# Cached-attention decode block: maxima per key group, shared normalisation, and work moved from TensorE to VectorE in ten queries

## The chip, the cores and the metric

The kernel runs on one core of a Trainium2 chip. The metric is the device time of one execution in microseconds (us), lower is better. Before the change the median of three runs is 1307.19 us (1306.52 to 1307.53).

## What is computed

A decoding step for two sequences (batch 2), model width 448: layer normalisation, attention of one new token per sequence over a cache of 8192 keys in 16 heads of 256, a residual sum, a second layer normalisation, a bilinear feed-forward layer of width 1792 and a second residual sum. All in 32-bit floats. Cut to what matters:

```python
q = (layernorm(x) @ wq).reshape(B, 1, 16, 256).transpose(0, 2, 1, 3)   # B = 2
scores = einsum("bhqd,bhkd->bhqk", q, k_cache) * 256 ** -0.5             # 8192 keys
o = einsum("bhqk,bhkd->bhqd", softmax(scores), v_cache)
h = x + o.transpose(0, 2, 1, 3).reshape(B, 1, 4096) @ wo
n = layernorm(h)
out = h + ((n @ w_gate) * (n @ w_up)) @ w_down
```

There are 32 pairs of a head and a sequence, called queries here and numbered i = 2 * head + sequence. Each has its own 8 MB of keys and 8 MB of values, which are read once: 537 MB in all, out of 561 MB that the kernel reads.

## The kernel before, in words

**Layout.** The 8192 keys of a query are cut into four groups of 2048. The key tile has the 128 partitions as one half of the head dimension (index `c` in 0, 1 for the two halves), then the four groups, then the 2048 keys of a group. The score tile `s` lies in PSUM as 128 x 2048: partitions 32g to 32g+31 hold group g, all 32 the same numbers, since the query is copied into 32 columns (`queries`, L193). The value tile `v` is 128 x 8 x 2048: partition 32g + r, slot o holds value dimension 32o + r of the keys of group g. So VectorE forms the output as a product of each slot with the 128 x 2048 tile of weights `p`, summed along the keys.

**Loop over the queries** (from L228). For each query i:

- SyncE (SP) issues the load of the keys (L84) into a buffer that exists once (`kbuf`, 64 KB a partition), then the load of the values (L91) into one of two buffers (`vbuf`). Each is one DMA of 8 MB. The issue of the next query's keys waits in SP's program until the last reader of the present keys is done, and what stands behind it on SP waits too.
- TensorE makes the scores (L206): four column tiles of 512 keys, two halves `c` and four groups, 32 matmuls of 128 x 32 weights; the four groups lie in four strips of the array's columns and run side by side. In the trace each 32-bit matmul is two records.
- VectorE takes the maximum along the 2048 keys (L242). TensorE turns the 128 numbers into a row (L244), VectorE takes their maximum (L246), TensorE spreads it to all partitions (L248), ScalarE copies it (L250). Only then ScalarE makes `p` = exp(s - max) and its sum (L252).
- VectorE forms the eight products with `v`, one instruction a slot (L259, SCALAR_TENSOR_TENSOR with an accumulator that is read out by a second, short instruction).
- After every second query `head_out` adds up the groups and divides by the sum of the weights for this head (L211 to L223); it stands behind the scores of the next query.

The tile framework turns every dependence between engines into a semaphore; each engine runs its own list in program order.

**Ends.** Before the loop come the first normalisation and the query projection out of `wq_t`, during which the first keys are under way. Behind the loop SP issues the loads of the output projection (`wo_t`, into the key buffer), gate and up weights (`gu_t`, into the value buffer of query 30) and down weights (`wd_t`, into that of query 31). The output projection, the second normalisation (L303 to L335) and the feed-forward layer follow. Gate and up products lie in banks 0 and 1 of one PSUM tile `ff`; the transposed products `hm_ps` in banks 2 and 0.

Of the kernel before, what the change touches and what calls it, by code (L numbers as in the profile page):

```python
# [20 lines left out]
GK = SK // G  # L21
# [15 lines left out]

WO_CUTS = (6, 11, 14, 15)


LAYOUT = (
    (slice(0, P), slice(0, DC - 1), slice(0, DC - 1)),
# [6 lines left out]
def tile_decode_block(  # L49
# [9 lines left out]
    wd: bass.AP,  # L59
    out: bass.AP,  # L60
):

# [46 lines left out]
    xr = const.tile([P, DC + 1, B, 16], F32, name="xr")  # L109
    nc.gpsimd.memset(xr[:, DC - 1 :], 0.0)  # L110
    oT = const.tile([P, H, 2, B], F32, name="oT")
    acc_ps = ps_1.tile([P, D], F32, name="acc_ps")
    nc.vector.memset(acc_ps, 0.0)

# [57 lines left out]

    qT = const.tile([P, 2, G, 2, 2, B], F32, name="qT")
    q_ps = ps_s.tile([P, 4, MM], F32, tag="s", name="q_ps")
    q_sb = one.tile([P, 2, MM], F32, tag="p", name="q_sb")
    for k in range(2):
        project(
            q_ps[:, k], wq_t, HD, (MM,) * 4, [k * BATCH + g * MM for g in range(4)],
# [9 lines left out]
            q_ps[:, 2 + k].rearrange("p (n g b r) -> p n g b r", n=4, g=G, b=B)[..., 0],  # L188
        )

    def queries(h):
# [9 lines left out]
    def scores(s, q, b, kt):  # L201
        for j in range(GK // MM):
            at = slice(j * MM, (j + 1) * MM)
            for c in range(2):
                for g in range(G):
                    nc.tensor.matmul(  # L206
                        s[g * R : (g + 1) * R, at], q[:, c, b, :], kt[:, c, g, at],
                        start=(c == 0), stop=(c == 1),
                    )

    def head_out(h, oacc, lsum):  # L211
        l_ps = ps_m.tile([P, B], F32, tag="sm", name=f"l_ps_{h}")
        nc.tensor.matmul(l_ps, ones, lsum, start=True, stop=True)  # L213
        rl = work.tile([P, B], F32, tag="rl", name=f"rl_{h}")
        nc.vector.reciprocal(rl, l_ps)  # L215
        oT_ps = ps_m.tile([P, B, 2], F32, tag="sm", name=f"oT_ps_{h}")
        for r in range(G):
            nc.tensor.matmul(
                oT_ps[r * R : (r + 1) * R], gsum, oacc[:, :, r::G], start=True, stop=True
            )  # L220
        nc.vector.tensor_mul(
            oT[:, h].rearrange("p c b -> p b c"), oT_ps, rl[:, :, None].to_broadcast([P, B, 2])
        )  # L223

    q_now = queries(0)
    last = None

    for i in range(NQ):  # L228
        h, b = divmod(i, B)
        kt = load_k(b, h)  # L230
        vt = load_v(b, h, 2 if i == NQ - 1 else 1)
        if b == 0:
            oacc = work.tile([P, B, NO], F32, tag="oacc", name=f"oacc_{h}")
            lsum = work.tile([P, B], F32, tag="lsum", name=f"lsum_{h}")

        s = ps_s.tile([P, GK], F32, tag="s", name=f"s_{i}")
        scores(s, q_now, b, kt)
        if last is not None:
            head_out(*last)
            last = None  # L240
        m = work.tile([P, 1], F32, tag="m", name=f"m_{i}")
        nc.vector.tensor_reduce(m, s, axis=AX.X, op=ALU.max)  # L242
# [9 lines left out]
        nc.scalar.activation(p, s, AF.Exp, bias=nb, scale=1.0, accum_out=lsum[:, b : b + 1])  # L252

        if b == B - 1 and h + 1 < H:
            q_now = queries(h + 1)

        for o in range(NO):
            v = vt[:, o, :]
            nc.vector.scalar_tensor_tensor(  # L259
                v, v, 1.0, p, op0=ALU.mult, op1=ALU.mult, accum_out=oacc[:, b, o : o + 1]  # L260
            )
        if b == B - 1:
            last = (h, oacc, lsum)
# [17 lines left out]
    g_ps, u_ps = ff[:, 0], ff[:, 1]  # L281
    hm_ps = [ff[:, at, : 2 * P].rearrange("p (n k) -> p n k", k=P) for at in (2, 0)]
    ya_ps, yb_ps = ff[:B, 3, :YC], acc_ps[32 : 32 + B, :YC]
    for t in (g_ps, u_ps):
        nc.vector.memset(t[2 * 32 :, FG[2] :], 0.0)
# [9 lines left out]
                )  # L295

    project_out(range(WO_CUTS[1]))
    head_out(*last)
# [77 lines left out]
def pack(np, inputs):  # L376


    x = np.asarray(inputs["A_x"]).reshape(B, D).T
    last = x[3 * P :]  # L380
    got = {
        "x": np.concatenate(
            [x[: 3 * P].reshape(3, P, B).transpose(1, 0, 2).reshape(P, 3 * B),
             np.concatenate([last, last], axis=0)], axis=1
        )
    }
    k = np.asarray(inputs["A_k_cache"]).reshape(B, H, SK, 2, P)
    got["kc"] = np.ascontiguousarray(k.transpose(0, 1, 4, 3, 2)).reshape(B, H, P, 2 * SK)
# [45 lines left out]
```

## Time and profile before

| | |
|---|---|
| median of 3 runs | 1307.19 us (1306.52 to 1307.53) |
| profiled execution: its time | 1306.09 us |
| profiled execution: span, first to last instruction | 1304.3 us |
| VectorE busy | 663.4 us (51% of the span) |
| TensorE matmuls busy | 365.3 us (28%) |
| ScalarE busy | 79.6 us (6%) |
| GpSimd busy | 0.8 us |
| mean granted TensorE clock | 0.631 of full speed |

Busy times come from one profiled execution. The profile cuts the span into 40 slices and gives each engine's busy share in tenths, the granted clock of TensorE in tenths of full speed, and what the 16 DMA engines moved. A group of instructions is listed with its line, engine and operation, the tiles it writes and reads (out<-in), how often it ran, its busy time and mean duration, then the idle time of the engine before it and what ended that. The timeline gives start, duration and the same names; the arrow behind a row tells how long the engine sat idle before it and what released it. "SPq" is a DMA issue on SyncE, "PEld" the weight load of TensorE.

### The profile page before, as it was taken

To read this page: it belongs to the slowest core of one execution; us is meant where nothing else is said; L and a number is where in the kernel's file an instruction comes from. 1 tells how busy PE (TensorE), PEld (TensorE's weight loads), DVE (VectorE), ACT (ScalarE), POOL (GpSimd) and SP (SyncE) were. 2 spreads that over 40 slices of the span, in tenths; PEclk is the share of its full clock that TensorE was granted. 3 is DMA by queue.
4 is the path that set the end of the run, shared out by engine and by line. 5 is a ranking of instruction groups with operands and counts; after the bars stand their busy time and mean duration, and the time that the engine had idled before them with its cause. 6 is when DMAs were issued, how large, how long until landed. Compare 5 with 4: busy or idle time off the path is not lost.

```text
span 1304.3 us, 6274 instructions
## 1 busy us (share of the span) xinstructions
PE 365.3 (28%) x2592; PEld 116.9 (9%) x2592; DVE 663.4 (51%) x648; ACT 79.6 (6%) x119; POOL 0.8 (0%) x7
## 2 busy tenths in 40 slices
PE   3333212332212233211232211323321233321247
PEld 1000000010000001000010000101000010100012
DVE  0246564445565445655444656444556544556552
ACT  0100000000000000000000000000000000000000
POOL 0000000000000000000000000000000000000000
PEclk9666566666556666656666655666655666655669
DMA  9999999999999999999999999999999999999998
GB/s 418 421 446 421 446 423 444 425 442 427 440 428 437 433 434 435 432 435 434 432 437 430 439 428 441 426 443 424 445 422 446 423 445 422 445 424 444 424 425 340
DMA packets 11841, 561.59 MB, mean 431 GB/s; under 512 B 1443, under 2 KB 1573, under 8 KB 2597
## 3 DMA queue, kind: packets, MB, share of 16 engines
q1 hardware_dynamic: 11668, 561.19, 99.5%
q8 instruction: 20, 0.33, 0.1%
q14 instruction: 9, 0.07, 0.0%
q10 hardware_dynamic: 144, 0.00, 0.0%
HBM read 561.19 MB, written 0.00 MB: 430 GB/s over the span
## 4 chain that ended last, share of the span: by engine, by line
DMA 75%; PE 24%; issue 0%; DVE 0%; SPq 0%; ACT 0%; ACTq 0%; DVEq 0%
DMA k<-in_kc_dram 73%; PE s L206 23%; DMA wo_t<-in_wo_dram 2%; PE ff_ps L167 1%; PE ff_ps L364 0%; SPq L267 0%; PE hT_ps L309 0%; PE acc_ps L292 0%; PE ff_ps L357 0%; PE l_ps L213 0%; DVE tail L353 0%; ACT tail L348 0%; DVE tail L303 0%; DVE xr L318 0%; PE acc_ps L341 0%
## 5 line engine op out<-in xcount | busy, mean ns | idle before, releaser
L259 DVE SCALAR_TENSOR_TENSOR v<-v,p 128x2048 f32<-128x2048 f32 x256 | 569.0, 2288 | 215.6 <-DMA v<-in_vc_dram 212.6
L206 PE MATMUL s<-k,q 128*32 128x512 f32 x2048 | 294.4, 739 | 804.2 <-DMA k<-in_kc_dram 804.2
L242 DVE TENSOR_REDUCE m<-s 128x1 f32<-128x2048 f32 x32 | 73.2, 2287 | 190.2 <-PE s L206 190.2
L206 PEld LDWEIGHTS s<-k,q 128*32 128x32 f32 x2048 | 80.9, 133 | 991.5 <-issue 991.5
L215 DVE RECIPROCAL rl<-l_ps 128x2 f32<-128x2 f32 x16 | 2.7, 171 | 166.7 <-PE l_ps L213 166.7
L250 ACT ACTIVATE nb<-nb_ps 128x1 f32<-128x1 f32 x32 | 5.5, 172 | 1148.3 <-PE nb_ps L248 1148.3
L252 ACT ACTIVATE p<-s,nb 128x2048 f32<-128x2048 f32 x32 | 63.0, 1968 | 1.0
L244 PE MATMUL mT<-ident,m 128*1 128x128 f32 x32 | 9.8, 306 | 79.4 <-DVE m L242 79.4
L259 DVE DVE_READ_ACCUMULATOR v<-v,p 128x1 f32 x256 | 21.3, 83 | 0.0
L248 PE MATMUL nb_ps<-nm,ones 1*128 1x1 f32 x64 | 15.2, 303 | 11.8 <-DVE nm L246 11.8
L246 DVE TENSOR_REDUCE nm<-mT 1x1 f32<-1x128 f32 x32 | 8.9, 278 | 12.7 <-PE mT L244 12.7
L248 PEld LDWEIGHTS nb_ps<-nm,ones 1*128 1x128 f32 x64 | 12.4, 241 | 19.1 <-DVE nm L246 19.1
L292 PE MATMUL acc_ps<-wo_t,oT 128*2 128x448 f32 x64 | 9.2, 632 | 14.6 <-DMA wo_t<-in_wo_dram 14.6
L244 PEld LDWEIGHTS mT<-ident,m 128*1 128x1 f32 x32 | 2.5, 79 | 96.1 <-DVE m L242 96.1
L167 PE MATMUL q_ps<-wq_t,xr 128*32 128x512 f32 x64 | 9.2, 727 | 2.3 <-DMA wq_t<-in_wq_dram 1.9
L167 PE MATMUL ff_ps<-gu_t,xr 128*32 128x384 f32 (+1 forms) x64 | 8.7, 633 | 0.9 <-ACT tail L348 0.9
L118 DVE TENSOR_REDUCE sum_h_x<-xT 128x2 f32<-128x6 f32 x1 | 0.2, 159 | 14.4 <-DMA xT<-in_x_dram 14.4
L186 DVE COPY qT<-q_ps 128x32 f32<-128x32 f32 x2 | 0.4, 191 | 12.0 <-PE q_ps L183 12.0
L252 ACT ACTIVATION_READ_ACCUMULATOR p<-s,nb 128x1 f32 x32 | 6.2, 193 | 0.0
L213 PE MATMUL l_ps<-lsum,ones 128*128 128x2 f32 x32 | 6.1, 262 | 0.0
L213 PEld LDWEIGHTS l_ps<-lsum,ones 128*128 128x128 f32 x32 | 4.8, 188 | 13.3 <-issue 13.3
L353 DVE TENSOR_TENSOR tail<-ff_ps,tail 128x256 f32<-128x256 f32 x2 | 0.8, 420 | 9.8 <-PE ff_ps L167 9.8
(69 smaller groups left out, 60.8 us busy)
## 6 DMA issues: line engine op xcount, KB each, us to landing
v<-in_vc_dram SPq DMA_DIRECT2D x2, 4096.0 KB, 37.8
wq_t<-in_wq_dram SPq DMA_DIRECT2D x1, 7168.0 KB, 19.4
wo_t<-in_wo_dram SPq DMA_DIRECT2D x1, 2688.0 KB, 16.2
wo_t<-in_wo_dram SPq DMA_DIRECT2D x1, 2240.0 KB, 21.2
gu_t<-in_B_w_gate_dram SPq DMA_DIRECT2D x1, 1792.0 KB, 28.9
gu_t<-in_B_w_up_dram SPq DMA_DIRECT2D x1, 1792.0 KB
wd_t<-in_wd_dram SPq DMA_DIRECT2D x2, 896.0 KB, 19.8
wo_t<-in_wo_dram SPq DMA_DIRECT2D x1, 1344.0 KB, 23.9
```

Of the source, the lines that this page charges most:

```text
L167: nc.tensor.matmul(ps[32 * g : 32 * g + 32, : wide[g]], xs.rearrange("p b r -> p (b r)"), w[:, at : at + wide[g]], start=(c == 0), stop=(c ...
L206: nc.tensor.matmul(s[g * R : (g + 1) * R, at], q[:, c, b, :], kt[:, c, g, at], start=(c == 0), stop=(c == 1),)
L213: nc.tensor.matmul(l_ps, ones, lsum, start=True, stop=True)
L215: nc.vector.reciprocal(rl, l_ps)
L242: nc.vector.tensor_reduce(m, s, axis=AX.X, op=ALU.max)
L244: nc.tensor.transpose(mT, m, ident)
L246: nc.vector.tensor_reduce(nm, mT, axis=AX.X, op=ALU.max, negate=True)
L248: nc.tensor.matmul(nb_ps, ones[0:1, :], nm, start=True, stop=True)
L250: nc.scalar.activation(nb, nb_ps, AF.Copy, scale=float(R))
L252: nc.scalar.activation(p, s, AF.Exp, bias=nb, scale=1.0, accum_out=lsum[:, b : b + 1])
L259: nc.vector.scalar_tensor_tensor(v, v, 1.0, p, op0=ALU.mult, op1=ALU.mult, accum_out=oacc[:, b, o : o + 1])
L292: nc.tensor.matmul(acc_ps[32 * j : 32 * j + B, :], oT[:, h, c, :], wo_t[:, k * D : (k + 1) * D], start=(h < 2), stop=(h >= H - 2),)
```

## The change

- **Maxima.** The maximum of a query's scores is no longer shared by the partitions. Each partition uses its own (equal for the 32 of a group), negated, kept in column i of `nm`; exp runs with it at once. The transposition, the second maximum, the spreading matmul and the copy of each query are gone.
- **Sums.** The sums of weights go to column i of `ls`, the unnormalised outputs to row i of `oacc`. Once after query 29 (for queries 0 to 29) and once after query 31 (for the last two) `weights` makes factors that bring the groups to a common maximum and divide by the sum; `weigh`, `turn` and `heads_out` apply them. `head_out` is gone.
- **Scores of ten queries.** In queries 1, 4, 7, ... 28 (`by_vector`) VectorE multiplies the second half (c = 1) of the keys by the query, a scalar for each partition, and adds the four pieces (one TENSOR_SCALAR, three SCALAR_TENSOR_TENSOR, each 128 x 2048, in place in the key tile). The host has packed that half with group and dimension exchanged, so that partition 32g + r holds dimension 32o + r of group g in piece o. Four matmuls with the 0/1 matrix `block` (128 x 128) then sum the 32 partitions of each group and add that to the scores of the first half, which TensorE makes as before.
- **Products with V.** In queries 0 to 29 the first n value slots (n = 4, 4, 8 for i mod 3 = 0, 1, 2) are multiplied by one wide TENSOR_TENSOR and summed by one wide TENSOR_REDUCE; the remaining slots keep the old instruction. Queries 30 and 31 keep it for all eight.
- **Tail.** The up product has a PSUM tile of its own (`u_ps`); `hm_ps` uses banks 2 and 1 of `ff`.

The core of the diff:

```diff
+EARLY = NQ - B
+WIDE = (4, 4, 8)
+
+def by_vector(i):
+    return i < EARLY and i % 3 == 1
...
+    block = const.tile([P, P], F32, name="block")
+    nc.gpsimd.memset(block, 0.0)
+    for g in range(G):
+        nc.gpsimd.memset(block[g * R : (g + 1) * R, g * R : (g + 1) * R], 1.0)
...
+    qd_ps = ps_m.tile([P, G, NQ], F32, tag="sm", name="qd_ps")
+    for o in range(G):
+        nc.tensor.matmul(
+            qd_ps[:, o, :].rearrange("p (n b) -> p n b", b=B),
+            spread[:, o].rearrange("p g r -> p (g r)"),
+            qT.rearrange("p k g j c b -> p (k g j) c b")[:, :, 1, :],
+            start=True, stop=True,
+        )
+    nc.vector.tensor_copy(qd, qd_ps)
...
+    def scores(s, q, i, kt):
+        upper = kt[:, 1]
+        if by_vector(i):
+            nc.vector.tensor_scalar(
+                upper[:, 0], upper[:, 0], qd[:, 0, i : i + 1], None, op0=ALU.mult
+            )
+            for o in range(1, G):
+                nc.vector.scalar_tensor_tensor(
+                    upper[:, 0], upper[:, o], qd[:, o, i : i + 1], upper[:, 0],
+                    op0=ALU.mult, op1=ALU.add,
+                )
+        tiles = [slice(j * MM, (j + 1) * MM) for j in range(GK // MM)]
+        for at in tiles:
+            for c in range(1 if by_vector(i) else 2):
...
+        if by_vector(i):
+            for at in tiles:
+                nc.tensor.matmul(
+                    s[:, at], block, upper[:, 0, at], start=False, stop=True,
+                    skip_group_check=True,
+                )
+
+    def weights(a, z):
+        n = z - a
+        nmT = ps_m.tile([n, P], F32, tag="sm", name=f"nmT_{a}")
+        nc.tensor.transpose(nmT, nm[:, a:z], ident)
+        low = work.tile([n, 1], F32, tag="low", name=f"low_{a}")
+        nc.vector.tensor_reduce(low, nmT, axis=AX.X, op=ALU.min)
+        diag = work.tile([n, n], F32, tag="diag", name=f"diag_{a}")
+        nc.vector.tensor_scalar(diag, ident[:n, :n], low, None, op0=ALU.mult)
+        all_ps = ps_m.tile([P, n], F32, tag="sm", name=f"all_ps_{a}")
+        nc.tensor.matmul(all_ps, ones[:n, :], diag, start=True, stop=True)
+        w = work.tile([P, n], F32, tag="w", name=f"w_{a}")
+        nc.vector.scalar_tensor_tensor(
+            w, all_ps, float(R), nm[:, a:z], op0=ALU.mult, op1=ALU.subtract
+        )
+        nc.scalar.activation(w, w, AF.Exp)
+        lw = work.tile([P, n], F32, tag="lw", name=f"lw_{a}")
+        nc.vector.tensor_mul(lw, ls[:, a:z], w)
+        l_ps = ps_m.tile([P, n], F32, tag="sm", name=f"l_ps_{a}")
+        nc.tensor.matmul(l_ps, ones, lw, start=True, stop=True)
+        rl = work.tile([P, n], F32, tag="rl", name=f"rl_{a}")
+        nc.vector.reciprocal(rl, l_ps)
+        nc.vector.tensor_mul(w, w, rl)
+        return w
...
-        m = work.tile([P, 1], F32, tag="m", name=f"m_{i}")
-        nc.vector.tensor_reduce(m, s, axis=AX.X, op=ALU.max)
-        mT = ps_m.tile([1, P], F32, tag="sm", name=f"mT_{i}")
-        nc.tensor.transpose(mT, m, ident)
-        nm = work.tile([1, 1], F32, tag="nm", name=f"nm_{i}")
-        nc.vector.tensor_reduce(nm, mT, axis=AX.X, op=ALU.max, negate=True)
-        nb_ps = ps_m.tile([P, 1], F32, tag="sm", name=f"nb_ps_{i}")
-        nc.tensor.matmul(nb_ps, ones[0:1, :], nm, start=True, stop=True)
-        nb = work.tile([P, 1], F32, tag="nb", name=f"nb_{i}")
-        nc.scalar.activation(nb, nb_ps, AF.Copy, scale=float(R))
+        nc.vector.tensor_reduce(nm[:, i : i + 1], s, axis=AX.X, op=ALU.max, negate=True)
...
+        if i == EARLY - 1:
+            w = weights(0, EARLY)
+        if i == NQ - 1:
+            w = weights(EARLY, NQ)
+
+        n = WIDE[i % 3] if i < EARLY else 0
+        if n:
+            v = vt[:, :n, :]
+            nc.vector.tensor_mul(v, v, p[:, None, :].to_broadcast([P, n, GK]))
+            nc.vector.tensor_reduce(oacc[:, i, :n], v, axis=AX.X, op=ALU.add)
+        for o in range(n, NO):
...
+    u_ps = ps_1.tile([P, MM], F32, name="u_ps")
+    hm_ps = [ff[:, at, : 2 * P].rearrange("p (n k) -> p n k", k=P) for at in (2, 1)]
```

**How the order of the instructions moves.** In the rows below the last number of a name is the tile's own; k_0 and k_1, v_0 and v_1 are the two sequences. The rows are those of queries 0, 1 and 2. The line numbers of the changed kernel are its own. On VectorE, behind the query projection, there stands before:

```order
L242 TENSOR_REDUCE m_216<-s_183 128x1
L246 TENSOR_REDUCE nm_220<-mT_218 1x1
L259 SCALAR_TENSOR_TENSOR v_0_179,oacc_181<-v_0_179,p_226 128x2048 x8
L242 TENSOR_REDUCE m_273<-s_240 128x1
L246 TENSOR_REDUCE nm_277<-mT_275 1x1
L259 SCALAR_TENSOR_TENSOR v_1_238,oacc_181<-v_1_238,p_283 128x2048 x8
L215 RECIPROCAL rl_336<-l_ps_334 128x2
L221 TENSOR_TENSOR oT<-oT_ps_338,rl_336 128x2x2
L242 TENSOR_REDUCE m_344<-s_301 128x1
```

And on VectorE after the change, for the same three queries:

```order
L321 TENSOR_REDUCE nm<-s_198 128x1
L340 TENSOR_TENSOR v_0_196<-v_0_196,p_232 128x8192
L341 TENSOR_REDUCE oacc<-v_0_196 128x4
L344 SCALAR_TENSOR_TENSOR v_0_196,oacc<-v_0_196,p_232 128x2048 x4
L243 TENSOR_SCALAR k_1_240<-k_1_240,qd 128x2048
L247 SCALAR_TENSOR_TENSOR k_1_240<-k_1_240,qd 128x2048 x3
L321 TENSOR_REDUCE nm<-s_244 128x1
L340 TENSOR_TENSOR v_1_242<-v_1_242,p_270 128x8192
L341 TENSOR_REDUCE oacc<-v_1_242 128x4
L344 SCALAR_TENSOR_TENSOR v_1_242,oacc<-v_1_242,p_270 128x2048 x4
L321 TENSOR_REDUCE nm<-s_284 128x1
L340 TENSOR_TENSOR v_0_282<-v_0_282,p_318 128x16384
```

The four instructions on the keys of query 1 (L243, L247) stand behind all products of query 0 and ahead of the maximum of query 1.

On TensorE, for queries 0 and 1 and the start of query 2, there stands before:

```order
L206 MATMUL s_183<-k_0_177,q_175 32x512 x32
L244 MATMUL mT_218<-ident,m_216 1x128
L248 MATMUL nb_ps_222<-nm_220,ones 128x1
L206 MATMUL s_240<-k_1_236,q_175 32x512 x32
L244 MATMUL mT_275<-ident,m_273 1x128
L248 MATMUL nb_ps_279<-nm_277,ones 128x1
L206 MATMUL s_301<-k_0_295,q_285 32x512 x32
```

After the change TensorE has there, up to query 4:

```order
L255 MATMUL s_198<-k_0_194,q_192 32x512 x32
L255 MATMUL s_244<-k_1_240,q_192 32x512 x16
L261 MATMUL s_244<-k_1_240,block 128x512 x4
L255 MATMUL s_284<-k_0_280,q_272 32x512 x32
L255 MATMUL s_326<-k_1_322,q_272 32x512 x32
L255 MATMUL s_374<-k_0_370,q_362 32x512 x16
L261 MATMUL s_374<-k_0_370,block 128x512 x4
```

In queries 1 and 4 the last readers of the key tile are now the four matmuls of L261, which read what VectorE has written into it.

More of the change, by code (lines that the diff above doesn't have):

```diff
@@ L174, in tile_decode_block @@
     q_ps = ps_s.tile([P, 4, MM], F32, tag="s", name="q_ps")
-    q_sb = one.tile([P, 2, MM], F32, tag="p", name="q_sb")
+    q_sb = one.tile([P, 3, MM], F32, tag="p", name="q_sb")
+    spread = q_sb[:, 2].rearrange("p (o g r) -> p o g r", o=G, g=G)
+    nc.vector.tensor_copy(
+        spread,
+        ident.rearrange("p (o r) -> p o r", r=R)[:, :, None, :].to_broadcast([P, G, G, R]),
+    )
     for k in range(2):
@@ L205, in scores @@
                 for g in range(G):
                     nc.tensor.matmul(
-                        s[g * R : (g + 1) * R, at], q[:, c, b, :], kt[:, c, g, at],
-                        start=(c == 0), stop=(c == 1),
-                    )
[L211 to L214, printed above, removed]
-        nc.vector.reciprocal(rl, l_ps)
-        oT_ps = ps_m.tile([P, B, 2], F32, tag="sm", name=f"oT_ps_{h}")
+                        s[g * R : (g + 1) * R, at], q[:, c, i % B, :], kt[:, c, g, at],
@@ L217, in head_out, with weigh, turn @@
+    def weigh(a, z, w):
+        nc.vector.tensor_mul(
+            oacc[:, a:z], oacc[:, a:z], w[:, :, None].to_broadcast([P, z - a, NO])
+        )
+    def turn(a, z):
+        oT_ps = ps_m.tile([P, z - a, 2], F32, tag="sm", name=f"oT_ps_{a}")
         for r in range(G):
             nc.tensor.matmul(
-                oT_ps[r * R : (r + 1) * R], gsum, oacc[:, :, r::G], start=True, stop=True
+                oT_ps[r * R : (r + 1) * R], gsum, oacc[:, a:z, r::G], start=True, stop=True
             )
-        nc.vector.tensor_mul(
-            oT[:, h].rearrange("p c b -> p b c"), oT_ps, rl[:, :, None].to_broadcast([P, B, 2])
+        return oT_ps
@@ L223, in head_out, with heads_out @@
+    def heads_out(a, z, oT_ps):
+        nc.vector.tensor_copy(
+            oT[:, a // B : z // B].rearrange("p h c b -> p h b c"),
+            oT_ps.rearrange("p (h b) c -> p h b c", b=B),
         )
     q_now = queries(0)
-    last = None
     for i in range(NQ):
@@ L243, in tile_decode_block @@
[L243 to L250 removed]
+        scores(s, q_now, i, kt)
@@ L251, in tile_decode_block @@
+        if i == EARLY:
+            oT_ps = turn(0, EARLY)
+        nc.vector.tensor_reduce(nm[:, i : i + 1], s, axis=AX.X, op=ALU.max, negate=True)
+        if i == EARLY:
+            heads_out(0, EARLY, oT_ps)
         p = one.tile([P, GK], F32, tag="p", name=f"p_{i}")
-        nc.scalar.activation(p, s, AF.Exp, bias=nb, scale=1.0, accum_out=lsum[:, b : b + 1])
+        nc.scalar.activation(
+            p, s, AF.Exp, bias=nm[:, i : i + 1], scale=1.0, accum_out=ls[:, i : i + 1]
+        )
         if b == B - 1 and h + 1 < H:
@@ L261, in tile_decode_block @@
             )
-        if b == B - 1:
-            last = (h, oacc, lsum)
+        if i == EARLY - 1:
+            weigh(0, EARLY, w)
+    weigh(EARLY, NQ, w)
     wo_t = kbuf.tile([P, H * WO], F32, tag="k", align_bytes=512, name="wo_t")
@@ L297, in tile_decode_block @@
     project_out(range(WO_CUTS[1]))
-    head_out(*last)
+    heads_out(EARLY, NQ, turn(EARLY, NQ))
     project_out(range(WO_CUTS[1], H))
@@ L387, in pack @@
     k = np.asarray(inputs["A_k_cache"]).reshape(B, H, SK, 2, P)
-    got["kc"] = np.ascontiguousarray(k.transpose(0, 1, 4, 3, 2)).reshape(B, H, P, 2 * SK)
+    kc = np.ascontiguousarray(k.transpose(0, 1, 4, 3, 2)).reshape(B, H, P, 2 * SK)
+    for h, b in (divmod(i, B) for i in range(NQ) if by_vector(i)):
+        upper = k[b, h, :, 1].reshape(G, GK, G, R).transpose(0, 3, 2, 1)
+        kc[b, h, :, SK:] = upper.reshape(P, SK)
+    got["kc"] = kc
     v = np.asarray(inputs["A_v_cache"]).reshape(B, H, G, GK, NO, R)
```

23 lines of the change are left out of this document (8 added, 15 removed).

## The prediction

> **What bounds the kernel now.** The page of the profile comes first: the DMA lines, then the chain of waits.
>
> ```profile
> span 1304.3 us, 6274 instructions
> ...
> DMA  9999999999999999999999999999999999999998
> ...
> q1 hardware_dynamic: 11668, 561.19, 99.5%
> ...
> DMA k<-in_kc_dram 73%; PE s L206 23%; DMA wo_t<-in_wo_dram 2%; PE ff_ps L167 1%; PE ff_ps L364 0%; SPq L267 0%; PE hT_ps L309 0%; PE acc_ps L292 0%; PE ff_ps L357 0%; PE l_ps L213 0%; DVE tail L353 0%; ACT tail L348 0%; DVE tail L303 0%; DVE xr L318 0%; PE acc_ps L341 0%
> ```
>
> The DMA engines work in every slice, SP's queue alone fills 99.5% of their time, and the chain consists of key transfers and the scores that release them. The kernel is a stream of bytes; compute matters only where it makes the stream stop. Whether it can is read from one period of the timeline.
>
> ```profile
> 504.70 9.15 PE L206 MATMUL s<-k,q 128*32 128x512 f32 x64 [25.23 <-DMA k<-in_kc_dram]
> ...
> 508.09 0.22 PEld L206 LDWEIGHTS s<-k,q 128*32 128x32 f32 x4 [0.63 <-issue]
> 508.94 0.14 PEld L206 LDWEIGHTS s<-k,q 128*32 128x32 f32 x4 [0.63 <-issue]
> 509.37 0.13 PEld L206 LDWEIGHTS s<-k,q 128*32 128x32 f32 x4 [0.29 <-issue]
> ...
> 513.90 0.33 SPq L84 DMA_DIRECT2D k<-in_kc_dram  x1
> ...
> 518.15 1.97 ACT L252 ACTIVATE p<-s,nb 128x2048 f32<-128x2048 f32 x1
> 520.02 0.19 ACT L252 ACTIVATION_READ_ACCUMULATOR p<-s,nb 128x1 f32 x1
> 523.97 2.29 DVE L259 SCALAR_TENSOR_TENSOR v<-v,p 128x2048 f32<-128x2048 f32 x1 [6.49 <-DMA v<-in_vc_dram]
> 526.19 0.08 DVE L259 DVE_READ_ACCUMULATOR v<-v,p 128x1 f32 x1
> 526.19 2.29 DVE L259 SCALAR_TENSOR_TENSOR v<-v,p 128x2048 f32<-128x2048 f32 x1
> ...
> 541.67 0.08 DVE L259 DVE_READ_ACCUMULATOR v<-v,p 128x1 f32 x1
> 543.34 8.60 PE L206 MATMUL s<-k,q 128*32 128x512 f32 x64 [25.43 <-DMA k<-in_kc_dram]
> ```
>
> Keys land at 504.70 and again at 543.34: the period is 38.64 us for 16.8 MB. The values land 19.27 us after the keys, at 523.97. The next keys are issued at 513.90, 9.2 us after the present ones landed and 10 us before the values are through, so the queue never runs dry. VectorE's products end at 541.75, before the next keys land. The release of the key buffer thus has a margin, and the change works on exactly that margin. What the margin is worth needs the time that a transfer takes from its issue on an empty queue; the kernel's last transfer (two rows of output) shows it, in the timeline and in SP's waits.
>
> ```profile
> 1302.01 0.33 SPq L370 DMA_DIRECT2D out_dram<-tail  x1
> ...
> SPq L430 <- DMA out_dram<-tail: 0.9, 1, 0.9
> ```
>
> 0.33 + 0.9 gives 1.2 to 1.3 us; I take 1.3. If keys are issued x after the last landing of keys, the queue stands still for x + 1.3 - 19.3 us where that is positive: the release may come 18.0 us after the landing. Before, it comes at 9.2.
>
> **The change part by part.** The durations come from the groups of the page, and from the groups kept apart by shape (second fence).
>
> ```profile
> L259 DVE SCALAR_TENSOR_TENSOR v<-v,p 128x2048 f32<-128x2048 f32 x256 | 569.0, 2288 | 215.6 <-DMA v<-in_vc_dram 212.6
> L206 PE MATMUL s<-k,q 128*32 128x512 f32 x2048 | 294.4, 739 | 804.2 <-DMA k<-in_kc_dram 804.2
> L242 DVE TENSOR_REDUCE m<-s 128x1 f32<-128x2048 f32 x32 | 73.2, 2287 | 190.2 <-PE s L206 190.2
> ```
>
> ```profile
> L353 DVE TENSOR_TENSOR tail<-ff_ps,tail 128x256 f32<-128x256 f32 x2 | 0.8, 420 | 9.8 <-PE ff_ps L167 9.8
> ```
>
> *Wide products.* VectorE takes 2288 ns for 2048 elements of two tensors and 420 ns for 256: (2288 - 420) / 1792 = 1.04 ns an element. No row shows 8192 elements; by this slope the wide multiplication of four slots takes 2.29 + 6144 x 1.04 ns = 8.7 us, that of eight 17.2 us. The reduction has L242 as its nearest row, 2287 ns for 2048 elements, the same price: 8.7 and 17.2 us. Four slots in the old way take 4 x 2.21 = 8.85 us (pitch 523.97 to 526.19). With 0.1 us for the dependence, the products of a query cost 26.3 us (n = 4) or 34.5 us (n = 8), against 17.8 us now. The bounds: a multiplication at half the price (the slope of a copy, below) is the second rival, a tenth dearer the third.
>
> *Keys on VectorE.* Three SCALAR_TENSOR_TENSOR, each needing the one before it, cost 3 x 2.32 = 7.0 us. For the TENSOR_SCALAR ahead of them there are two neighbours: the two-tensor row, 2.29 us, and a copy with one source in SBUF, in the timeline beside a small product.
>
> ```profile
> 1282.62 0.17 DVE L137 TENSOR_TENSOR sq_h<-xc_h 128x8 f32<-128x8 f32 x1
> ...
> 1283.21 0.23 DVE L323 COPY tail<-sum_sq_h 128x128 f32<-128x128 f32 x1
> ```
>
> The copy takes 0.06 us more for 120 elements more, 0.5 ns each. A scalar product has one tensor to read, as the copy has; so I take 0.17 + 2040 x 0.5 ns = 1.2 us and keep 2.3 as the other end. Together 8.2 us, at most 9.3. The Trainium skill ("VectorE: DVE Perf Modes", section on the perf-mode tier table) lets a 32-bit tensor_scalar out of SBUF run at two elements a cycle, 1227 ns for 2048, but tensor_tensor and tensor_reduce at one. By the dearer row the sum below would be 47 us in place of 36.
>
> *Block matmuls.* Four matmuls of 512 columns over the whole array replace 16 that ran four side by side: two records each, so 8 sets of 512 columns, as many as before. A set takes 0.85 us (508.09 to 508.94) after a pause and 0.43 us (508.94 to 509.37) later. All 16 sets of a query take 294.4 / 32 = 9.2 us; without eight sets of 0.43 that is 5.8 us. TensorE will be cold for them: the first half needs 5.8 us from the landing, then it waits some 10 us for VectorE, and the windows of the trace show the granted clock (the column before the DMA share) back at half 8 us after the scores end at 513.8.
>
> ```profile
> 515.00:518.00 3.00, 0.65 (x3) 0.37 (x3) 2.12 (x2) 0.05 (x1) 0.00 (x0) 1.00 0.87 371
> 518.00:521.00 3.00, 0.00 (x0) 0.00 (x0) 0.00 (x0) 2.18 (x3) 0.00 (x0) 0.69 1.06 459
> 521.00:524.00 3.00, 0.00 (x0) 0.00 (x0) 0.03 (x1) 0.00 (x0) 0.00 (x0) 0.50 1.01 437
> ```
>
> The bounds are 3.4 us (all at 0.43) and 6.8 us (all at 0.85). The Trainium skill ("TensorE: Matmul & The Clock Gate", Part 1) gives 3.4 us of sustained work until the full clock; by that, four sets of 0.85 and four of 0.43, 5.1 us, and 29 us in place of 36 below. The trace disagrees a little: the long sets last 4.2 us here.
>
> *The sum.* Call the queries of a triple A, B, C (i mod 3 = 0, 1, 2), with zero where A's keys land. C's products before it began when its values landed, at 19.3 - 38.6 = -19.3, and end at +15.2. VectorE then takes A's maximum, to 17.5; ScalarE needs 1.97 + 0.19 us, to 19.7; A's values landed at 19.3. A's products run from 19.7 to 46.0. B's keys landed at 38.6, but in VectorE's order they stand behind A's products: 46.0 to 54.2. Block matmuls to 60.1; the issue of C's keys at 60.2. That is x = 21.6 us after B's landing, where 18.0 was allowed: the stream stands still for 3.6 us. Queued behind the waiting issue on SP are C's values, whose buffer was free at 46.0; they lose nothing more. Behind the key work on VectorE stands B's own maximum; B's products begin near 64.6 and end near 91; C's keys land at 80.9, its scores are done at 90.1, and its products begin with the landing of its values at 100.2. So the next triple starts from the same state. For A and C the key buffer is still released by TensorE alone, 9.2 us after landing. Ten triples have a B; in the first no C runs ahead and A starts at 19.3, so 3.2: 9 x 3.6 + 3.2 = 35.6, say 36 us. With every unknown at its cheap end (block 3.4) each stop is 1.2, in all 12 us; at its dear end (block 6.8, TENSOR_SCALAR 2.3) 5.7, in all 57 us.
>
> *What costs nothing.* The removed maximum chain of each query lay ahead of the landing of the values (exp is done at 520.21, values at 523.97): no gain. In the last query it did count:
>
> ```profile
> 1251.04 2.29 DVE L242 TENSOR_REDUCE m<-s 128x1 f32<-128x2048 f32 x1 [10.91 <-PE s L206]
> ...
> 1254.95 1.97 ACT L252 ACTIVATE p<-s,nb 128x2048 f32<-128x2048 f32 x1
> ...
> 1257.04 2.29 DVE L259 SCALAR_TENSOR_TENSOR v<-v,p 128x2048 f32<-128x2048 f32 x1 [2.97 <-ACT p L252]
> ...
> 1275.66 0.16 DVE L221 TENSOR_TENSOR oT<-oT_ps,rl 128x4 f32<-128x4 f32 x1
> ...
> 1278.09 0.92 PE L292 MATMUL acc_ps<-wo_t,oT 128*2 128x448 f32 x4 [0.26 <-DMA wo_t<-in_wo_dram]
> ...
> 1292.98 0.16 PEld L167 LDWEIGHTS ff_ps<-gu_t,xr 128*32 128x32 f32 x8 [0.76 <-DMA gu_t<-in_B_w_up_dram]
> ```
>
> From the end of the maximum to the products 3.7 us pass. In the new order exp takes 2.2 of these and the second `weights`, eight short steps of 0.2 to 0.5 us, ends about 1.4 behind it: the same. The product that `weigh` adds (0.2 us) delays the last head to 1275.9, while its weights land at 1278.1. Without that cover it would cost its 0.2. The first `weights` (some 3 us with its hand-overs) comes in query 29 after exp, about 14 us behind the landing of the keys; its values land at 19.3. The preparation of `qd` lies ahead of the first keys: 7 us of waiting there.
>
> ```profile
> 32.72 0.19 DVE L186 COPY qT<-q_ps 128x32 f32<-128x32 f32 x1 [5.17 <-PE q_ps L183]
> 39.63 1.93 PE L206 MATMUL s<-k,q 128*32 128x512 f32 x8 [7.01 <-DMA k<-in_kc_dram]
> ```
>
> The up product's own bank frees it of a wait for the gate's copy, but its last third waits for its weights until 1292.98 anyway; at most 0.5 us, set at nothing.
>
> So the profiled execution, 1306.1 us, becomes 1341.7; the median of the runs stood 1.1 above it: 1343 us.
>
> **The rivals.** *In time (no change).* If VectorE is quicker than extrapolated, so that x stays below 18.0, nothing is lost. The point lies 3.6 us lower; one multiplication of 8192 at the copy's slope (8192 x 0.5 = 4.1 us instead of 8.7) passes it alone. Then the time is the old one, 1307 us. For: only short rows bear the extrapolation. Against: a multiplication reads two tensors, like L259 and L353, and these agree at 1.04. *Faster.* Between the landings at 39.63 and at 1241.68
>
> ```profile
> 39.63 9.62 PE s L206 x64
> ...
> 1241.68 9.33 PE s L206 x64
> ```
>
> (chain of waits, in order of time) 31 periods take 38.78 us each, 0.14 more than the undisturbed one: 4 us of hiccups in the stream. If the release is in time and fewer instructions to fetch take half of that and the up bank 0.5 us, 1304.5 us. The stream itself gets no faster, since its bytes stay the same; nothing in the profile ties the hiccups to instructions. *Dearer.* Wide operations a tenth dearer than the slope move A's start by 3.4 us and A's end by 5.1, each stop grows from 3.6 to 8.7 us, and the time goes to about 1390. Strided or long accesses could do that; no row does. *That the change doesn't do what it says* is excluded for the order: the rows above show the key work behind A's products.
>
> **How the numbers follow.** Forecast with its bounds (1318 to 1364): 0.74. In time: 0.16. Dearer: 0.06. Faster: 0.04. The forecast's own range leaves 0.26 out, so the range reaches to the case in time, with the low end at 1305.5 for the scatter of the runs: 1305.5 to 1364. About 0.2%, 2.6 us, is what a measurement can tell from no change: slower 0.80, same 0.16, faster 0.04.
>
> **What would show it.** In the changed profile: SP's issue of the keys behind each B query at 21 to 22 us after B's landing; ten distances between landings of 42.2 us instead of 38.64, 20 of the others unchanged; a DMA share below nine tenths in slices that hold a stop; wide products of 8.7 and 17.2 us; block matmuls of 5 to 6.5 us at a clock of half at their start. Wrong it would be if x stays under 18, or if stops appear behind A or C, or if VectorE's products hold up the values.

## The result, and the profile after

The changed kernel takes 1366.52 us (median of 5 runs, 1363.42 to 1369.18) against 1307.15 before: 1.0455 times as long, 95% interval 1.0438 to 1.0472. The direction and the place were forecast; the time lies 23.5 us above the forecast and 2.5 us above the range. The profiled execution took 1366.04 us, its span is 60.0 us longer than that of before. The page after, the lines that answer to those quoted of before:

```profile
span 1364.3 us, 5042 instructions
...
PE 363.5 (27%) x2130; PEld 110.7 (8%) x2130; DVE 1071.2 (79%) x382; ACT 74.3 (5%) x89; POOL 1.4 (0%) x12
...
DMA  9989998999899899989989998998999899989998
...
q1 hardware_dynamic: 11668, 561.19, 95.7%
...
DMA k<-in_kc_dram 33%; DMA v<-in_vc_dram 21%; PE s L255 9%; DVE v L340 7%; DVE v L344 6%; DVE oacc L341 6%; DVE k L247 5%; PE s L261 5%; DMA gu_t<-in_B_w_up_dram 2%; DMA wo_t<-in_wo_dram 1%; DVE k L243 1%; DVE nm L321 0%; PE ff_ps L451 0%; ACT p L325 0%
```

The bytes are the same, but the queue is busy for 95.7% instead of 99.5%; the ten eights among the DMA slices that the page before does not have are the stops, and VectorE, at 0% of the chain before, now holds a quarter of it. One stop in the timeline, queries 13 (B), 14 (C) and the landing of 15:

```profile
567.65 5.99 PE L255 MATMUL s<-k,q 128*32 128x512 f32 x32 [28.66 <-DMA k<-in_kc_dram]
...
574.73 1.28 DVE L243 TENSOR_SCALAR k<-k,qd 128x2048 f32<-128x2048 f32 x1
576.05 7.13 DVE L247 SCALAR_TENSOR_TENSOR k<-k,qd 128x2048 f32<-128x2048 f32 x3
583.24 5.10 PE L261 MATMUL s<-k,block 128*128 128x512 f32 x8 [9.60 <-DVE k L247]
588.37 0.33 SPq L99 DMA_DIRECT2D k<-in_kc_dram  x1
...
610.14 8.66 PE L255 MATMUL s<-k,q 128*32 128x512 f32 x64 [21.80 <-DMA k<-in_kc_dram]
...
618.86 0.33 SPq L99 DMA_DIRECT2D k<-in_kc_dram  x1
...
649.70 9.36 PE L255 MATMUL s<-k,q 128*32 128x512 f32 x64 [30.90 <-DMA k<-in_kc_dram]
```

B's keys land at 567.65; VectorE comes to them only at 574.73, when A's products are done; TensorE waits 9.6 us for it; the keys of C are issued at 588.37, x = 20.7 us after the landing. They land 21.8 us later, 42.5 us behind B's. In the windows (the last two columns are the DMA share and GB/s; a packet counts where it starts, so the share can exceed 1) nothing starts around that issue:

```profile
585.00:586.00 1.00, 1.00 (x3) 0.38 (x2) 0.00 (x0) 0.00 (x0) 0.00 (x0) 0.50 0.01 0
586.00:588.30 2.30, 2.30 (x6) 0.79 (x4) 0.00 (x0) 0.00 (x0) 0.00 (x0) 0.98 0.00 0
588.30:589.30 1.00, 0.03 (x1) 0.00 (x0) 0.93 (x1) 0.00 (x0) 0.00 (x0) 1.00 0.00 0
589.30:590.30 1.00, 0.00 (x0) 0.00 (x0) 1.00 (x1) 0.00 (x0) 0.00 (x0) 1.00 3.11 1049
```

By the packet records the last engine ends the old values at 586.39 and the first starts the new keys at 589.32, so all 16 stand still for 2.9 us here; over the ten stops it is 2.8 to 4.5 us, 3.8 on average, and nowhere else in the stream of keys and values do all of them stand still.

The new operations, in the groups by shape, cost what the rows of before had given:

```profile
L340 DVE TENSOR_TENSOR v<-v,p 128x8192 f32<-128x8192 f32 x20 | 173.8, 8692 | 57.9 <-DMA v<-in_vc_dram 29.5 <-ACT p L325 28.4
L341 DVE TENSOR_REDUCE oacc<-v 128x4 f32<-128x8192 f32 x20 | 173.7, 8686 | 0.7
L340 DVE TENSOR_TENSOR v<-v,p 128x16384 f32<-128x16384 f32 x10 | 172.3, 17225 | 78.8 <-DMA v<-in_vc_dram 78.8
...
L247 DVE SCALAR_TENSOR_TENSOR k<-k,qd 128x2048 f32<-128x2048 f32 x30 | 70.5, 2352 | 1.1
...
L261 PE MATMUL s<-k,block 128*128 128x512 f32 x80 | 61.9, 946 | 97.7 <-DVE k L247 97.7
...
L243 DVE TENSOR_SCALAR k<-k,qd 128x2048 f32<-128x2048 f32 x10 | 12.8, 1283 | 0.0
```

**Where the 60 us lie.** The landing of the keys is the first score matmul of a query in the timeline; from the landing of query 0 to that of query 31 pass 1261.8 us, 59.8 more than before (1202.1). Their 31 distances, read from those rows:

| | before | after | times | difference |
|---|---|---|---|---|
| from B's landing to C's | 38.67 us | 43.59 us | 10 | 49.3 us |
| the other distances | 38.83 us | 39.33 us | 21 | 10.5 us |

So five sixths lie in the distances that hold a stop (of their 4.9 us each, 3.8 are the standstill), and one sixth in distances in which no release is late.

### The profile page after: what moved, and what is told of

Its sections match the earlier page's. It is cut to its first block, busy times and chain, and to the rows that moved or that the text cites. A ratio compares the mean times of both kernels' runs of the same rounds, so it can differ in the third digit from the quotient of the medians.

```text
span 1364.3 us, 5042 instructions
## 1 busy us (share of the span) xinstructions
PE 363.5 (27%) x2130; PEld 110.7 (8%) x2130; DVE 1071.2 (79%) x382; ACT 74.3 (5%) x89; POOL 1.4 (0%) x12
## 3 DMA queue, kind: packets, MB, share of 16 engines
q1 hardware_dynamic: 11668, 561.19, 95.7%
## 4 chain that ended last, share of the span: by engine, by line
DMA 57%; DVE 25%; PE 15%; issue 2%; another core or an unknown queue 1%; ACT 0%; SPq 0%; DVEq 0%; ACTq 0%
DMA k<-in_kc_dram 33%; DMA v<-in_vc_dram 21%; PE s L255 9%; DVE v L340 7%; DVE v L344 6%; DVE oacc L341 6%; DVE k L247 5%; PE s L261 5%; DMA gu_t<-in_B_w_up_dram 2%; DMA wo_t<-in_wo_dram 1%; DVE k L243 1%; DVE nm L321 0%; PE ff_ps L451 0%; ACT p L325 0%
## 5 line engine op out<-in xcount | busy, mean ns | idle before, releaser
L255 PE MATMUL s<-k,q 128*32 128x512 f32 x1728 | 257.1, 759 | 843.8 <-DMA k<-in_kc_dram 843.8
L340 DVE TENSOR_TENSOR v<-v,p 128x8192 f32<-128x8192 f32 (+1 forms) x30 | 346.1, 11537 | 136.7 <-DMA v<-in_vc_dram 108.3
L341 DVE TENSOR_REDUCE oacc<-v 128x4 f32<-128x8192 f32 (+1 forms) x30 | 345.9, 11531 | 1.0
L344 DVE SCALAR_TENSOR_TENSOR v<-v,p 128x2048 f32<-128x2048 f32 x96 | 214.0, 2287 | 2.1 <-ACT p L325 2.1
L321 DVE TENSOR_REDUCE nm<-s 128x1 f32<-128x2048 f32 x32 | 73.2, 2288 | 87.5 <-PE s L261 63.0
L325 ACT ACTIVATE p<-s,nm 128x2048 f32<-128x2048 f32 x32 | 63.0, 1967 | 1194.3 <-DVE nm L321 1194.3
L261 PE MATMUL s<-k,block 128*128 128x512 f32 x80 | 61.9, 946 | 97.7 <-DVE k L247 97.7
L247 DVE SCALAR_TENSOR_TENSOR k<-k,qd 128x2048 f32<-128x2048 f32 x30 | 70.5, 2352 | 1.1
L261 PEld LDWEIGHTS s<-k,block 128*128 128x128 f32 x80 | 23.9, 313 | 135.6 <-DVE k L247 96.4
L243 DVE TENSOR_SCALAR k<-k,qd 128x2048 f32<-128x2048 f32 x10 | 12.8, 1283 | 0.0
L344 DVE DVE_READ_ACCUMULATOR v<-v,p 128x1 f32 x96 | 8.0, 83 | 0.0
```

The costliest lines, as they stand in the source:

```text
L243: nc.vector.tensor_scalar(upper[:, 0], upper[:, 0], qd[:, 0, i : i + 1], None, op0=ALU.mult)
L247: nc.vector.scalar_tensor_tensor(upper[:, 0], upper[:, o], qd[:, o, i : i + 1], upper[:, 0], op0=ALU.mult, op1=ALU.add,)
L255: nc.tensor.matmul(s[g * R : (g + 1) * R, at], q[:, c, i % B, :], kt[:, c, g, at], start=(c == 0), stop=(c == 1), skip_group_check=True,)
L261: nc.tensor.matmul(s[:, at], block, upper[:, 0, at], start=False, stop=True, skip_group_check=True,)
L321: nc.vector.tensor_reduce(nm[:, i : i + 1], s, axis=AX.X, op=ALU.max, negate=True)
L325: nc.scalar.activation(p, s, AF.Exp, bias=nm[:, i : i + 1], scale=1.0, accum_out=ls[:, i : i + 1])
```

## The experiments

Two theories stood against each other ("release" is the issue of the next keys, counted from the landing of the present ones). *Late release*: nothing but the release of the key buffer in the ten B queries matters; the queue runs dry, and what follows is the price of starting it again. *Load*: VectorE at four fifths busy slows the stream by itself. All kernels are the changed kernel with one edit.

### Without the key work on VectorE

```diff
 def by_vector(i):
-    return i < EARLY and i % 3 == 1
+    return False
```

> The change without the part on the keys: by_vector is always false, so TensorE makes all scores and the key buffer is released by TensorE alone; maxima per group, shared sums and the wide products (4, 4, 8) stay. Late release (the stream stops only because the keys' release waits for VectorE in ten queries): no stop, 1306 to 1308 us, release 9 us after every landing. Load (VectorE at four fifths busy slows the stream by itself, in proportion to its extra busy time, 59 us for 408): busy near 985 us, so 1307 + 59 x 322 / 408 = 1354 us.

Measured: 1305.96 us, 0.9994 of before (0.9985 to 1.0004), with VectorE busy for 988.9 us. No loss is left, though VectorE does 326 us more than before. That speaks for the late release and against load.

### Without the wide products

```diff
-WIDE = (4, 4, 8)
+WIDE = (0, 0, 0)
```

> The change without the wide products: all eight slots in the old instruction, the key work of ten queries stays. Late release: the products of the query before end ahead of the landing, so the key work starts at the landing and the release comes 8.5 + 6 = 14.5 us after it, under the 16.7 from which the stream would stop: 1306 to 1308 us. If the key work alone were the cause (any wait of the release on VectorE costs a stop): 1330 us or more. Load: busy near 745 us, 1319 us.

Measured: 1305.81 us, 0.9993 (0.9983 to 1.0002). The releases come 13.3 us after the landing on average. The key work alone is free, too: the loss needs both parts of the change at once.

### The wide products elsewhere

```diff
-WIDE = (4, 4, 8)
+WIDE = (0, 8, 8)
```

> The same amount of work as in the change, elsewhere: wide slots (0, 8, 8) instead of (4, 4, 8), so that none stand ahead of the key work. VectorE's busy time stays near 1071 us. Late release: key work starts at the landing, release near 14.6 us, no stop, 1306 to 1308 us. Load: 1366 us as the change.

Measured: 1304.94 us, 0.9986 (0.9977 to 0.9996). Its page:

```profile
span 1303.5 us, 5022 instructions
...
PE 359.4 (28%) x2130; PEld 108.1 (8%) x2130; DVE 1069.2 (82%) x362; ACT 74.3 (6%) x89; POOL 1.4 (0%) x12
...
DMA  9999999999999999999999999999999999999998
```

VectorE is as busy as in the change (1069 against 1071 us) and no slice but the last has an eight, as before. Load is excluded: what counts is only that the four wide slots stand ahead of the key work. The release comes at 13.9 us. This is the one kernel whose interval lies below the kernel before, by 0.14%, less than the 0.2% that the prediction took as the least that can be told from no change.

### Two wide slots, and six

```diff
-WIDE = (4, 4, 8)
+WIDE = (2, 4, 8)
```

> Two wide slots instead of four ahead of the key work (2, 4, 8): release near 21.6 - 4.1 = 17.5 us after the landing. With the prediction's limit of 18.0 us: no stop, 1307 us. With a limit of 16.7 us (a transfer into an empty queue takes 22.0 us from issue to landing instead of 20.6): ten short stops of 0.9 us, and behind each a visible delay of about 1 us: 1317 to 1326 us.

Measured: 1324.11 us, 1.0132 (1.0116 to 1.0149). The releases come at 16.4 to 18.1 us, 17.3 on average, eight of the ten under the prediction's limit of 18.0, and still the ten distances are 39.73 us on average. One of them, queries 10 and 11 with the issue between:

```profile
433.15 5.23 PE L255 MATMUL s<-k,q 128*32 128x512 f32 x32 [30.11 <-DMA k<-in_kc_dram]
...
450.92 0.33 SPq L99 DMA_DIRECT2D k<-in_kc_dram  x1
...
472.90 2.79 PE L255 MATMUL s<-k,q 128*32 128x512 f32 x12 [22.02 <-DMA k<-in_kc_dram]
```

A release at 17.8 us makes a distance of 39.75. The limit was too high; 16.7 us, that is 38.6 less the 22.0 us that a restarted transfer takes, fits eight of the ten to 0.3 us. The other two (41.1 and 41.2) take 24.3 us from issue to landing: by the packet records one or two of the 16 engines begin the keys 2.2 to 2.9 us after the first, and why they do is not shown.

```diff
-WIDE = (4, 4, 8)
+WIDE = (6, 4, 8)
```

> Six wide slots instead of four ahead of the key work (6, 4, 8): VectorE's work there grows by 4.1 us, so the release moves from 21.6 to 25.7 us after the landing. Late release: each of the ten stops grows by that amount, nothing else changes: 1366 + 41 = 1407 us. Load: busy time grows by 41 us of 408, so by 6 us: 1372 us.

Measured: 1407.02 us, 1.0758 (1.0743 to 1.0772). The release moves to 25.65 us (21.63 in the change), B's distance to 47.83 us (43.59): 4.0 us later, 4.2 us longer, ten times. Behind the limit the time follows the release nearly one for one; load would have given 6 us.

### Five stops instead of ten

```diff
 def by_vector(i):
-    return i < EARLY and i % 3 == 1
+    return i < EARLY and i % 6 == 1
```

> Key work on VectorE in five queries (1, 7, 13, 19, 25) instead of ten; all else as in the change. Late release: five stops, each with what follows it, half of 59 us: 1336 to 1338 us; without a stop the distances between landings are 38.6 us. Load: busy time falls by 42 us of 408: 1360 us.

Measured: 1336.38 us, 1.0219 (1.0205 to 1.0233): half the loss. The cost belongs to the stops, some 6 us for each.

### The key buffer in two halves

```diff
-        t = kbuf.tile([P, 2, G, GK], F32, tag="k", align_bytes=512, name=f"k_{h}_{b}")
-        nc.sync.dma_start(t.rearrange("p c g k -> p (c g k)"), kc[b, h])
-        return t
+        halves = []
+        for c in range(2):
+            t = kbuf.tile([P, G, GK], F32, tag=f"k{c}", align_bytes=256, name=f"k{c}_{h}_{b}")
+            nc.sync.dma_start(
+                t.rearrange("p g k -> p (g k)"), kc[b, h, :, c * SK : (c + 1) * SK]
+            )
+            halves.append(t)
+        return halves
```

(The output weights, which use the same buffer later, are two tiles likewise.)

> The change with the key buffer as two tiles of half the size, one for each half of the head dimension, each loaded by its own DMA (and the output weights in two tiles likewise). In the ten queries the first half is free after TensorE's part, 6 us after the landing, and its next load keeps the queue filled for 9.7 us more while the second half waits for VectorE until 21.6 us. VectorE and TensorE do the same work at the same places. Late release: no stop, 1306 to 1309 us. Load: 1366 us.

Measured: 1306.7 us, 0.9995 (0.9985 to 1.0004), with the wide products and the key work in the same places as in the change. One B query in its timeline:

```profile
559.58 5.16 PE L266 MATMUL s<-k,block 128*128 128x512 f32 x8 [19.42 <-DVE k L252]
564.78 0.33 SPq L101 DMA_DIRECT2D k<-in_kc_dram  x1
...
573.14 1.94 PE L260 MATMUL s<-k,q 128*32 128x512 f32 x8 [8.39 <-DMA k<-in_kc_dram]
...
582.73 8.04 PE L260 MATMUL s<-k,q 128*32 128x512 f32 x56 [7.66 <-DMA k<-in_kc_dram]
```

The second half is still released late (its issue stands at 564.78, behind the block matmuls), but C's first half is on its way by then and lands at 573.14; the second lands 9.6 us behind it, at the stream's pace. A late release costs nothing as long as other bytes are queued.

### Key work in all thirty queries

```diff
-WIDE = (4, 4, 8)
+WIDE = (0, 0, 0)
 def by_vector(i):
-    return i < EARLY and i % 3 == 1
+    return i < EARLY
```

> Key work on VectorE in all thirty queries, no wide products: each release near 14.5 us after the landing, under the limit; VectorE busy near 910 us. Late release: no stop; and with a quarter fewer TensorE instructions, some 13 or 14 fetches of instructions instead of 20, so at most two instead of three visible delays of 1.4 us: 1305 to 1307 us. Load: 1307 + 59 x 247 / 408 = 1343 us.

Measured: 1306.83 us, 0.9998 (0.9989 to 1.0007). No stop, as expected; that fewer reads of instructions (13 on queue 8 instead of 20; see below) would save a microsecond or more was not seen.

### What comes behind a stop

The 10.5 us in the other distances were in no theory yet. The distances behind a stop are of two kinds. Queries 20, 21 and 22 of the changed kernel (first matmuls of each), and the queues in that stretch:

```profile
854.62 9.30 PE L255 MATMUL s<-k,q 128*32 128x512 f32 x64 [21.82 <-DMA k<-in_kc_dram]
894.53 9.82 PE L255 MATMUL s<-k,q 128*32 128x512 f32 x64 [30.61 <-DMA k<-in_kc_dram]
933.14 2.79 PE L255 MATMUL s<-k,q 128*32 128x512 f32 x12 [28.79 <-DMA k<-in_kc_dram]
```

```profile
q1 hardware_dynamic: 576, 33.55, 98.7%
q8 instruction: 1, 0.02, 0.1%
q14 instruction: 1, 0.01, 0.0%
```

39.91 and 38.61 us: one is long, one is not. Queue 8 moves pieces of 16 KB, and their number goes with TensorE's records: 20 for 5184 before, 17 for 4260 in the change, 31 for 7876 in the last kernel below. So I read them as TensorE's instructions. The Trainium skill ("Runtime: NRT & Kernel Launch", section on the mechanics of instruction fetch) gives 256 instructions to a piece of 16 KB; these counts agree. In the packet records such a read holds one of the 16 DMA engines up by 0.9 us, and the next key or value packet on that engine takes 0.5 us longer. Of the 21 distances without a late release in the changed kernel, the 11 with such a read last 39.86 us on average, the 10 without 38.74: nine of these 38.6 to 38.7, and one 39.56, in which a smaller read on queue 14 (8 KB) is the first behind the stop. Before the change there are 20 such reads, yet most distances with one stay at 38.6.

The theory, *alignment*: in a running stream the 16 engines are apart from each other, the landing waits for the one that is furthest behind, and a read on any other engine is hidden. A stop sets all engines to nearly the same place, so the first read behind it shows in full.

The packet records bear this out. The ends of the 16 engines' shares of a transfer lie 0.4 to 1.0 us apart where a restarted transfer lands, and 1.4 to 2.0 us from the first read on queue 8 behind it on. Before the change they lie 0.5 us apart at query 0, where the stream has just begun, and 1.7 to 4.5 us from query 1 on. The first distance of all, ahead of any stop, fits as well: 39.7 to 40.2 us in the kernels with one key tile and a read in it, 38.64 in the one without (the next kernel).

Two kernels vary the number of reads and keep the ten stops.

```diff
-WIDE = (4, 4, 8)
+WIDE = (4, 0, 0)
 def by_vector(i):
-    return i < EARLY and i % 3 == 1
+    return i < EARLY
```

> Key work in all thirty queries, and four wide slots in queries 0, 3, 6, ... alone, so that the ten releases of the change stay late (near 21.7 us) and the others come near 14.8, under the limit; a fifth fewer TensorE instructions, so some 13 reads of instructions instead of 17. Alignment (a stop sets all 16 DMA engines to the same place, so that the first read of instructions behind it, which holds one engine up by 1.4 us, delays the next landing by as much; without a stop the other engines' later reads hide it): the two distances behind a stop add up to 77.3 us where no read falls into the triple and to 78.7 where one does; 1360 to 1366 us. If what comes behind a stop has nothing to do with reads of instructions: 78.7 us in every triple, 1366 us.

Measured: 1358.06 us, 1.0391 (1.0371 to 1.0412), with 13 reads on queue 8. Queries 20, 21 and 22 again, and the queues between them:

```profile
851.83 5.86 PE L255 MATMUL s<-k,q 128*32 128x512 f32 x32 [22.07 <-DMA k<-in_kc_dram]
...
891.00 5.06 PE L255 MATMUL s<-k,q 128*32 128x512 f32 x32 [23.79 <-DMA k<-in_kc_dram]
...
929.62 5.79 PE L255 MATMUL s<-k,q 128*32 128x512 f32 x28 [24.76 <-DMA k<-in_kc_dram]
```

```profile
q1 hardware_dynamic: 576, 33.55, 99.6%
q14 instruction: 1, 0.01, 0.0%
```

No read on queue 8 between the restart and the third landing, and the two distances add up to 77.8 us (39.17 + 38.62) where the changed kernel has 78.5. Of the ten triples five have no such read: 77.7 to 77.9; four of the five with one are at 78.4 to 78.9. In the fifth (77.8) a read on queue 14 had already fallen into the restarted transfer, which there takes 22.6 us instead of 22.0, and the read on queue 8 behind it adds only 0.5 us. So the delay goes with the read, by 0.8 us on average rather than the 1.4 expected, since the triples without a read do not come down to 77.3. In four of those five a smaller read on queue 14 makes part of the difference; in the one without any read (77.7) all 16 engines are late alike, and why stays open. The total is 2 us under the expected range, since the releases come 0.3 us earlier than in the change.

```diff
-        tiles = [slice(j * MM, (j + 1) * MM) for j in range(GK // MM)]
+        tiles = [slice(j * 256, (j + 1) * 256) for j in range(GK // 256)]
```

> The change with score and block matmuls of 256 columns instead of 512, so twice as many TensorE instructions there and some 31 reads of instructions instead of 17, nearly one in every distance between landings; the streaming time of TensorE stays the same. Alignment: only the first read behind a stop is visible, as the following ones fall on other engines: the two distances behind a stop still add up to 78.7 us (up to 79.2), 1366 to 1370 us if the releases stay where they are. If every read behind a stop cost 1.4 us: 80 us or more, 1380 us.

(This kernel does not compute the block's output any more. Two tiles now share a PSUM bank, so that in the ten queries sums of the first half are presumably lost there, which is not shown. Instructions and transfers are those that the expectation names.) Measured: 1370.98 us, 1.0482 (1.0458 to 1.0507), with 31 reads on queue 8. Queries 20, 21 and 22:

```profile
859.67 9.45 PE L255 MATMUL s<-k,q 128*32 128x256 f32 x128 [21.91 <-DMA k<-in_kc_dram]
899.70 9.91 PE L255 MATMUL s<-k,q 128*32 128x256 f32 x128 [30.57 <-DMA k<-in_kc_dram]
938.36 5.91 PE L255 MATMUL s<-k,q 128*32 128x256 f32 x64 [28.75 <-DMA k<-in_kc_dram]
```

78.7 us for the two distances with two reads; over the ten triples 78.2 to 78.8, mostly two reads each, the same as with one in the change (78.2 to 78.9). The second read behind a stop is hidden, as alignment has it; a price for every read would have given 80. The 4.5 us above the change go with the releases, 22.2 us after the landing instead of 21.6.

## Why the prediction was wrong

| step | predicted | measured |
|---|---|---|
| wide multiplication, 8192 and 16384 | 8.7, 17.2 us | 8.69, 17.23 us |
| wide reduction, 8192 | 8.7 us | 8.69 us |
| TENSOR_SCALAR; one SCALAR_TENSOR_TENSOR on keys | 1.2; 2.32 us (the latter from no row) | 1.28; 2.35 us |
| block matmuls of a query | 5.8 us | 6.2 us (61.9 / 10) |
| release after B's landing | 21.6 us | 21.63 us (mean of ten) |
| issue to landing on an empty queue | 1.3 + 19.3 = 20.6 us | 21.96 us (mean of ten) |
| distance B to C | 42.2 us | 43.59 us |
| other distances | as before, 38.8 us | 39.33 us |

**Right:** the mechanism, its place and, within 0.4 us, every term on the engines. The bound is the stream; the key work stands behind A's wide products; the release is late in B and nowhere else; the values hold nothing up (their issues wait for VectorE ten times, by up to 6.2 us, and no standstill follows); the removed maximum chain, the new tail and the shared sums cost and save, in sum, nothing that could be measured (without the key work the rest of the change is at 0.9994).

**Luck:** that the release agrees to 0.03 us. Counted from A's landing, C's keys are issued 61.1 us later and not 60.2, since A's values land later and the key work and block matmuls are a little dearer; but B's keys land 39.5 us behind A's and not 38.6, as in seven of the ten triples a read of instructions falls between them. The two errors cancel.

**Wrong, a size:** the step "what the margin is worth". The latency was read from the last transfer, two rows of output, as "1.2 to 1.3 us; I take 1.3", and added to the 19.3 us that 8 MB take in a running stream. A restarted transfer of 8 MB takes 22.0. The packet records show where the 1.4 us go. The first bytes flow 0.96 us after the issue, and the first matmul starts 0.47 us behind the last packet: together 1.4, near the 1.3 that was taken. But between them lie 20.5 us, not 19.3: the engines start up to 1.1 us apart, and their first packets take 3.1 us on average (2.4 to 3.5) instead of 2.42. Ten times 1.36 is 13.6 us. It also moves the limit from 18.0 to 16.7, which the kernel with two wide slots shows.

**Wrong, a term that was missing:** "So the next triple starts from the same state" held for VectorE but not for the DMA engines, which start a triple aligned. "For A and C the key buffer is still released by TensorE alone" was true, and their distances grew all the same: 10.5 us. The hiccups in the stream had been seen in the profile before (0.14 us a period) and dismissed, with "nothing in the profile ties the hiccups to instructions"; the trace of before does tie them: its five distances above 38.7 us (38.95 to 40.19) each hold a read on queue 8 or 14. The change has fewer such reads on queue 8 (17 instead of 20), but its stops made their delays visible. 35.6 + 13.6 + 10.5 = 59.7, the measured 59.8.

The range was built from the unknown prices on the engines, all of which came out near the taken values; the two terms of the DMA side had no bounds of their own, and both fell on the same side. Either one alone would have left the time inside the range (1343 + 13.6 or + 10.5); together they put it 2.5 us above. Of the rivals, *in time* failed at its condition (the long multiplication costs what the slope says), *faster* with it, and *dearer* was not what made the time longer.

**Open:** what makes the engines' start after a stop uneven and their first packets slow; what delays all 16 engines alike in a triple without a read; why the kernel with the moved wide products is 0.14% under the kernel before (fewer reads of instructions could be a reason, but the kernel with key work in all thirty queries, which has fewer still, does not show it).

## What to carry to other kernels

In a kernel that is one stream of bytes, price a change by the latest moment at which each buffer may be released, and list all that stands ahead of the last reader on every engine that reads it: here 406 to 408 us of added VectorE work cost nothing or 59 us, depending only on four wide slots ahead of the key work. A stop costs more than its length: add the restart (here 1.4 us) and the hidden delays that it uncovers (here 1 us). The remedy need not be less work: work in another place, as with the moved wide products, or other bytes in the queue, as with the split buffer, took the whole loss away.

## What the runs showed of the hardware

- A 32-bit TENSOR_TENSOR and TENSOR_REDUCE out of the value tile cost 1.04 ns an element between 8192 and 16384 elements (8692 and 17225 ns, 8686 and 17220 ns); a TENSOR_SCALAR with a scalar for each partition took 1283 ns for 2048, against 2352 ns for a SCALAR_TENSOR_TENSOR of that length.
- A stream from one queue holds 38.6 us for 16.8 MB, 434 GB/s, whether VectorE is busy for 663 us or for 1070.
- An 8 MB transfer that is issued on an empty queue lands after 22.0 us; in a running stream it adds 19.3.
- A read of instructions delays one of the 16 DMA engines by 1.4 us (0.9 for itself, 0.5 on the next packet). In a running stream this is mostly hidden, since the engines are 1.7 to 4.5 us apart anyway (before the change); behind a stop, where they are 0.4 to 1.0 us apart, the first such read shows and the second does not (78.2 to 78.8 us for two distances with two reads, 78.2 to 78.9 with one).
